# The experts' stage of a retention and mixture-of-experts kernel, written as a list of single steps per expert

## The chip, the cores and the metric

The kernel runs on one core of a Trainium2 chip. The core has TensorE for matmuls (PE in the profile, with its weight loads as PEld), VectorE (DVE), ScalarE (ACT), GpSimd (POOL) and SyncE (SP), which here only issues DMAs. Each engine works through its own queue in order, and an instruction that waits holds up everything behind it in its queue. SBUF holds the operands; PSUM, with eight banks of 512 floats per partition, takes the results of matmuls. The metric is the device time of one execution in microseconds (us).

## The reference

Retention attention over 8 batches, 8 heads, 576 tokens of 64 elements gives a matrix x of 4608 tokens by 512. Each token then goes to the one expert of eight whose embedding it is most like, and the output is that expert's two-layer network, scaled by the gate:

```
scores = (q @ k.T) / 8;  ret = scores * gamma_h ** (i - j) (j <= i, else 0);  x = ret @ v
logits = (x / |x|) @ (emb / |emb|).T / tau
idx = argmax(logits);  gate = softmax(logits)[idx]
for e in range(8):
    m = idx == e
    h = relu(x[m] @ w1[e])            # 512 -> 1024
    out[m] = gate[m] * (h @ w2[e])    # 1024 -> 512
```

All of it is float32.

## The kernel before

**Stages.** Attention and routing come first, batch after batch. Then the experts follow one after another, each with a capacity of 640 tokens in five tiles of 128. Expert 0's first layer is multiplied plainly; the experts 1 to 7 use Strassen's seven products with the tokens in two halves. A last part for tokens beyond capacity runs only if there are any.

**Precision.** Each float32 operand of the experts is split in two: ScalarE writes the rounded high part, and another engine then subtracts it from the source for the low part. A product is three matmuls, high by high, high by low and low by high. So each weight and each activation costs a ScalarE copy and a subtraction.

**An expert.** Its tokens are gathered by an indirect DMA that GpSimd issues (`gather`, line 404). `xturn` (453) lays the two 16-bit halves of each float apart on VectorE (457) and SyncE starts a transposing DMA (458); `xjoin` (462) joins them again on ScalarE (465) and forms the differences for Strassen in three VectorE instructions (479). `xput_b` and `xput_t` split the two results into `xsb` and `xst` (429, 430). The first layer's weights come in four loads; `sums1` forms block sums (218, four VectorE instructions) and `part1` splits them (226 and 227) into one of three slots. The second layer's weights come in four loads too, and `split2` splits them (191 and 192): the subtraction stands on GpSimd for experts 1 to 7.

**Rounds.** The first layer runs in four rounds. `round_a(r)` issues products 1 and 5 of block r and products 7 and 3 of block r-1; `round_b(r)` issues 6 and 2 of r and 4 of r-1. Products share banks: ScalarE copies bank z to x (1099), q to SBUF (1100) and z to v (1103) in between, and VectorE adds (1104, 1114). Each finished half goes through `out_half`: ScalarE's Relu (981), then VectorE's low part (982). A z bank is used by every other round, so it must be read to the end by then.

**Second layer.** `mm2` (1000) makes one tile of 128 tokens from 24 matmuls of 512 columns. `mm2_out` scales it by the gate on ScalarE (1013) and GpSimd scatters it with an indirect DMA (1017). Tiles 0 to 4 use banks m, o, m, o, m. Tile 4's matmuls are split: half of them before the next expert's `round_a(0)` and half behind it.

**Order.** From expert 0's second layer on, under `tc.manual_schedule()`, each engine takes instructions in the order in which the code is written. Work for the next expert is put between the rounds through the lists `bg`, `bg0`, `bg1`, `ahead` and `fill`. Buffers named raw are seven, for gathers, weight loads and block sums alike; a load or gather waits until one is free. Attention's part is ordered by a scheduler.

Of the kernel before, what the change touches and what calls it, by code (L numbers as in the profile page):

```python
# [9 lines left out]
F32 = mybir.dt.float32  # L10
# [3 lines left out]
U16 = mybir.dt.uint16  # L14
# [36 lines left out]
S1, S2, S3, S4, A11, A12, A22 = range(7)  # L51
PRODUCTS = {
# [54 lines left out]
def retention_moe(ctx: ExitStack, tc: tile.TileContext, qk, kv, embT, tau, w1, w2, cst, out):  # L107
# [344 lines left out]

    def xturn(e, i):

        t = xg[e, i]
        far = t[:, XO : XO + DM]
        nc.vector.tensor_copy(planes(far), words(t[:, :DM]))  # L457
        nc.sync.dma_start_transpose(
            out=t[:, :DM].bitcast(U16).rearrange("p (c n) -> p c n", n=P), in_=far.bitcast(U16)
        )  # L460

    def xjoin(e, i):
# [3 lines left out]
        if e == 0:  # L466
            return
        u = t[:, XO : XO + DM].rearrange("p (d n j) -> p d n j", d=NP, n=2)
        v = t[:, :DM].rearrange("p (k d n j) -> p k d n j", k=2, d=2, n=2)
        for o, x, y in (  # L470
# [8 lines left out]
            nc.vector.tensor_tensor(out=o, in0=x, in1=y, op=ALU.subtract)  # L479

# [486 lines left out]
    with ExitStack() as moe:  # L967
# [108 lines left out]
        def split2(e, c):  # L1076

            w_split(raws.pop((e, 1, c)), 1, c, nc.gpsimd if e else nc.vector)
# [15 lines left out]
        def round_a(e, r, width, bg=()):  # L1094

            products(e, width, [(1, r), (5, r)] * (r < 4) + [(7, r - 1), (3, r - 1)] * (r > 0))
            if r < 4:
                z, q = bank["z"][r % 2], half5[:, r % 2]
                nc.scalar.copy(bank["x"][:, :HALF], z[:, :HALF])  # L1099
                nc.scalar.copy(q, bank["q"][:, :HALF])  # L1100
            if r > 0:
                z, q = bank["z"][1 - r % 2][:, :HALF], half5[:, 1 - r % 2]
                nc.scalar.copy(bank["v"][:, :HALF], z)
                nc.vector.tensor_tensor(out=z, in0=z, in1=q, op=ALU.add)  # L1104
                for f in bg:
                    f()
                out_half(4 + r - 1, 1, z)
                out_half(r - 1, 1, bank["y"])

        def round_b(e, r, width, bg0=(), bg1=()):  # L1110

            products(e, width, [(6, r), (2, r)] * (r < 4) + [(4, r - 1)] * (r > 0))
            if r < 4:
                nc.vector.tensor_tensor(
                    out=bank["y"][:, :HALF], in0=bank["z"][r % 2][:, :HALF], in1=half5[:, r % 2], op=ALU.add
                )
            for f in bg0:
                f()
            if r < 4:
                out_half(r, 0, bank["x"])  # L1120
            if r > 0:
                out_half(4 + r - 1, 0, bank["v"])
            for f in bg1:
                f()
# [17 lines left out]
        for f in range(4, NF):  # L1142
            done = mm1_out(f, 0, mm1_in(f, 0))
            with after(*done):
                if f == 4:
                    gates()
                elif f == 5:
                    gates_out()
                    xturn(0, 3)
                    xturn(0, 4)  # L1150
                    gather(1, 0)
                elif f == 6:
                    count_beyond()
                    gather(1, 1)
                elif f == 7:
                    gather(1, 2)
                    gather_gates(0)
                split2(0, f - 4)

        with tc.manual_schedule():  # L1160
            ps = mm2(0, 0, fs=range(NF))
            xjoin(0, 3)
            xput_b(0, 3)
            xjoin(0, 4)
            xput_b(0, 4)
            gather(1, 3)
            gather(1, 4)
            gather_gates(1)
            for i in range(3):
                xturn(1, i)  # L1170
            load(1, 0, 0)
            mm2_out(0, 0, ps)
            ps = mm2(0, 1, fs=range(NF))
            for i in (3, 4):
                xturn(1, i)
            for i in (0, 1):
                xjoin(1, i)
                xput_t(1, i)
# [299 lines left out]
```

## Time and profile before

| | us |
|---|---|
| median of 3 runs | 672.48 (667.14 to 675.56) |
| the profiled execution | 673.74 |
| its span, first to last instruction | 671.9 |
| PE busy | 595.1 (89%) |
| DVE busy | 469.4 (70%) |
| ACT busy | 327.7 (49%) |
| POOL busy | 252.0 (38%) |
| mean granted clock of TensorE | 0.958 |

In the profile a line such as L1099 is that line of the kernel before. An entry "A <- B" says that A waited and B ended the wait. Matmuls overlap by about 0.16 us at the seams of the timeline's groups, so a group's cost is the distance from its start to the next group's start. Expert 0's second layer starts at 191.6 us, expert 1's first product at 238.9, and the experts 2 to 7 start at 298.6, 359.9, 422.1, 480.9, 544.6 and 606.2. The last tile of the expert that starts at 422.1 holds too few tokens to need its 24 matmuls, and they are skipped.

### The profile page before, as it was taken

Reading aid. Unit: us, or ns where it says so; the run is one execution under the profiler, and the core shown is the slowest. Engines: PE = TensorE matmul, PEld = TensorE weight load, DVE = VectorE, ACT = ScalarE, POOL = GpSimd, SP = SyncE. Lnnn points to the kernel's source line nnn. Section 1 sums busy time; section 2 is a strip of 40 time slices with the busy share of each in tenths; the row PEclk is TensorE's granted clock in tenths of the full one; section 3 lists DMA queues with packets and bytes.
Section 4 is the critical chain, followed back from the end, with each engine's and each line's share of the span. In section 5 each row is a group of like instructions: output and inputs, shape, how many; then the busy total and the mean of one; then the engine's idle time right before and its main releaser. Section 6 shows DMA issues by size and latency. Waiting matters only on the chain. (4 is left out here: it accounts for less than half of the span.)

```text
span 671.9 us, 13104 instructions
## 1 busy us (share of the span) xinstructions
PE 595.1 (89%) x5081; PEld 514.6 (77%) x5081; DVE 469.4 (70%) x966; ACT 327.7 (49%) x581; POOL 252.0 (38%) x193
## 2 busy tenths in 40 slices
PE   8999999997996898897889698987969897989796
PEld 7778778776886797687768686975768687769685
DVE  5676778787584878776886869577767859685700
ACT  1034324323563664664395457546734855575411
POOL 1422210221365045066325715650572257053311
PEclk9999999999999797999999898989989898989899
DMA  8898988847256255453734546364545344562001
GB/s 306 316 328 306 364 322 298 306 158 234 82 131 153 75 188 128 105 185 114 142 99 160 127 96 202 116 101 114 182 107 130 125 145 125 95 214 78 1 32 42
DMA packets 73299, 109.75 MB, mean 163 GB/s; under 512 B 44631, under 2 KB 45051, under 8 KB 71424
## 3 DMA queue, kind: packets, MB, share of 16 engines
q1 hardware_dynamic: 65536, 88.63, 42.9%
q0 software_dynamic: 7680, 19.95, 10.1%
q8 instruction: 60, 0.98, 0.6%
q14 instruction: 23, 0.19, 0.1%
HBM read 79.96 MB, written 19.94 MB: 149 GB/s over the span
## 5 line engine op out<-in xcount | busy, mean ns | idle before, releaser
L1000 PE MATMUL m<-wslot,hs 128*128 128x512 f32 (+1 forms) x888 | 209.7, 393 | 16.2 <-ACT y L1013 12.2
L1000 PEld LDWEIGHTS m<-wslot,hs 128*128 128x128 f32 x888 | 164.7, 192 | 55.4 <-ACT y L1013 14.8
L1017 POOL DMA_INDIRECT out<-y,sid x40 | 43.2, 1079 | 232.5 <-ACT y L1013 172.4
L1051 PE MATMUL a<-xst,wslot 128*128 128x292 f32 (+2 forms) x504 | 90.1, 323 | 20.3 <-ACT o L1099 14.3
L1051 PEld LDWEIGHTS a<-xst,wslot 128*128 128x128 f32 x504 | 79.5, 206 | 25.2 <-ACT o L1099 15.7
L227 DVE TENSOR_TENSOR wslot<-raw,wslot 128x768 fp32r<-128x768 f32 (+1 forms) x56 | 80.6, 1458 | 4.0 <-ACT wslot L226 3.7
L457 DVE COPY raw<-raw 128x1024 uint16<-128x1024 uint16 x37 | 53.9, 1458 | 36.9 <-DMA raw<-xd,gid 36.9
L192 POOL TENSOR_TENSOR wslot<-raw,wslot 128x1024 fp32r<-128x1024 f32 x28 | 66.7, 2400 | 21.0 <-ACT wslot L191 20.8
L658 POOL TENSOR_TENSOR vt<-vt,cs 128x512 f32<-128x512 f32 x28 | 28.4, 1046 | 87.5 <-DMA vt<-kv 57.5
L408 POOL DMA_INDIRECT raw<-xd,gid x40 | 47.3, 1182 | 33.5 <-DVE raw L690 20.3
L226 ACT CAST wslot<-raw 128x768 fp32r<-128x768 f32 (+1 forms) x56 | 50.6, 940 | 16.0 <-DVE raw L218 16.0
L419 POOL DMA_INDIRECT gt<-gd,gid x40 | 50.0, 1251 | 12.2 <-issue 10.7
L465 ACT COPY raw<-raw 128x1024 uint16<-128x1024 uint16 x37 | 49.8, 1347 | 4.4 <-DMA raw<-raw 4.4
L129 PE MATMUL a<-qkt 64*128 64x128 f32 (+1 forms) x640 | 46.9, 275 | 3.1 <-DVE raw L690 1.8
L479 DVE TENSOR_TENSOR raw<-raw 128x128 f32<-128x128 f32 (+1 forms) x105 | 35.3, 336 | 16.5 <-ACT raw L465 13.7
L129 PEld LDWEIGHTS a<-qkt 64*128 64x128 f32 (+1 forms) x640 | 38.3, 176 | 9.1 <-DVE raw L690 3.0
L690 DVE TENSOR_TENSOR raw<-a,tri 128x512 f32<-128x512 f32 x64 | 41.3, 681 | 5.5 <-PE a L129 5.4
L981 ACT ACTIVATE hs<-a 128x320 fp32r<-128x320 f32 (+2 forms) x44 | 19.1, 437 | 52.6 <-DVE a L1104 43.7
L1013 ACT ACTIVATE y<-m,gt 128x512 f32<-128x512 f32 (+1 forms) x38 | 25.7, 676 | 39.0 <-PE m L1000 38.8
L218 DVE TENSOR_TENSOR raw<-raw 128x256 f32<-128x256 f32 x112 | 42.4, 420 | 1.7 <-DMA raw<-w 0.6
L1051 PE MATMUL a<-xsb,wslot 128*128 128x292 f32 (+2 forms) x168 | 28.5, 305 | 13.0 <-DVE hs L982 12.3
L129 PE MATMUL a<-xsb,wslot 128*128 128x384 f32 (+1 forms) x192 | 31.7, 325 | 8.5 <-DVE hs L982 8.5
(164 smaller groups left out, 982.2 us busy)
## 6 DMA issues: line engine op xcount, KB each, us to landing
raw<-w SPq DMA_DIRECT2D x64, 512.0 KB, 4.5
qkt<-qk SPq DMA_DIRECT2D x32, 576.0 KB, 6.7
xd<-y SPq DMA_DIRECT2D x36, 256.0 KB, 3.1
vt<-kv SPq DMA_DIRECT2D x7, 1152.0 KB, 9.7
kt<-kv SPq DMA_DIRECT2D x7, 1024.0 KB, 5.2
vt<-kv SPq DMA_DIRECT2D x4, 256.0 KB, 7.9
raw<-xd,gid POOLq DMA_INDIRECT x40, 4.3
gt<-gd,gid POOLq DMA_INDIRECT x40, 3.7
```

Source lines behind the costliest of these rows:

```text
L129: pe[:] = [nc.tensor.matmul(*args, **kw)]
L192: (eng or nc.vector).tensor_tensor(out=sl[:, 1, c * 1024 : (c + 1) * 1024], in0=raw, in1=hi.bitcast(F32), op=ALU.subtract)
L218: nc.vector.tensor_tensor(out=o, in0=x, in1=y, op=op)
L226: nc.scalar.copy(sl[:, 0, b0:b1], src)
L227: nc.vector.tensor_tensor(out=sl[:, 1, b0:b1], in0=src, in1=sl[:, 0, b0:b1].bitcast(F32), op=ALU.subtract)
L408: return nc.gpsimd.indirect_dma_start(out=t[:, :DM], out_offset=None, in_=xd[:rows, :], in_offset=bass.IndirectOffsetOnAxis(ap=gid[:, a : ...
L419: nc.gpsimd.indirect_dma_start(out=g[:, i : i + 1], out_offset=None, in_=gd[:, :], in_offset=bass.IndirectOffsetOnAxis(ap=gid[:, a : a + 1 ...
L457: nc.vector.tensor_copy(planes(far), words(t[:, :DM]))
L465: nc.scalar.copy(words(t[:, XO : XO + DM]), planes(t[:, :DM]))
L1000: nc.tensor.matmul(ps[:, :step], hs[:, hsp, f, i * P : (i + 1) * P], w[:, ws, f, n : n + step], start=(part[0] and f == fs[0] and k == 0), ...
L1017: nc.gpsimd.indirect_dma_start(out=out[:, :], out_offset=bass.IndirectOffsetOnAxis(ap=sid[:, a : a + 1], axis=0), in_=y, in_offset=None, b ...
L1051: nc.tensor.matmul(ps[:, :n], w[:, ws, blk, d], x[:, xsp, d0 + d, half, :n], start=(new and d == 0 and k == 0), stop=(d == 1 and k == 2), ...
```

## The change

Rounds and background lists are replaced by three texts of words, `FIRST` (from expert 0's second layer to expert 1), `SECOND` (expert 1) and `SCHED` (experts 2 to 7). `walk` goes through a text, and `step` issues one word's instructions: A and B the products of a round, cx, cq, cv the copies, sy, sz the sums, h.. and l.. ScalarE's high part and VectorE's low part of one piece, a the block sums, M.. the second layer's matmuls, y the scaled output. A + marks work for the next expert: g a gather, u the laying apart, d its transposing DMA, j the joining, s the differences, w and v weight loads, G the gathers of gates. What used to be issued together, a high part and its low part, or u and d, is now placed word by word.

Besides the order, three things change. `split2`'s subtractions go to VectorE for all experts. The five output tiles use banks m, o, x, v, m. And the three first-layer banks are cleared only from column 292 on.

```diff
+SCHED = """
+A0 +g0 a3 cx0 Mz4 cq0 h20 h22 l20 B0 l22 yz4 +g1 h21 sy0 +g2 A1 hx0 lx0 l21 cx1 +g3 h23 cq1 l23 cv0
+sz0 +g4 B1 hz0 hy0 lz0 ly0 sy1 hx1 +u0 +d0 A2 hv0 hr3 lx1 cx2 lv0 hs3 lr3 cq2 cv1 sz1 B2 hz1 ls3 hy1
...
-            w_split(raws.pop((e, 1, c)), 1, c, nc.gpsimd if e else nc.vector)
+            w_split(raws.pop((e, 1, c)), 1, c)
...
+        def minus(out, x, y):
+
+            nc.vector.tensor_tensor(out=out, in0=x, in1=y.bitcast(F32), op=ALU.subtract)
...
+            elif k in ("h2", "l2"):
+                raw = raws[e, 1, i]
+                h, l = w2_parts(i, raw)
+                if k == "h2":
+                    nc.scalar.copy(h, raw)
+                else:
+                    minus(l, raw, h)
+                    del raws[e, 1, i]
+            elif k in MPART:
+                fs, part = MPART[k]
+                o = e - (k == "Mz")
+                ps = bank["moxvm"[i]]
+                mm2(o, i, ps, fs, part, wide[o] if i == CT - 1 and o else None)
...
-                ps = mm2(e, 2, bank["m"])
-                mm2_out(e, 2, ps)
...
+                for t in (*bank["z"], bank["q"]):
+                    nc.vector.memset(t[:, WIDTHS[0] : HALF], 0.0)
...
+        def walk(text, e):
+
+            for word in text.split():
+                (step if e or word[0] == "+" else opening)(word, *[e] * (e > 0 or word[0] == "+"))
...
         with tc.manual_schedule():
+            walk(FIRST, 0)
             for e in range(1, NE):
+                walk(SCHED if e > 1 else SECOND, e)
+                if e < NE - 1:
+                    walk("Mc4", e)
```

**VectorE in the first rounds of an expert.** This is VectorE's queue from the first sum of an expert's round 0 before; slots named wslot_84 and wslot_2771 hold the first layer's weights, and the COPY is the laying apart for the next expert.

```order
L1114 TENSOR_TENSOR m<-a,half_2772 128x320
L1034 UNCONDITIONAL_BRANCH
L982 SCALAR_TENSOR_TENSOR hs<-o,hs 128x5x64
L218 TENSOR_TENSOR raw<-raw 128x256 x4
L1034 UNCONDITIONAL_BRANCH
L1104 TENSOR_TENSOR a<-a,half_2772 128x320
L982 SCALAR_TENSOR_TENSOR hs<-a,hs 128x5x64
L982 SCALAR_TENSOR_TENSOR hs<-m,hs 128x5x64
L1114 TENSOR_TENSOR m<-a,half_2772 128x320
L457 COPY raw<-raw 128x1024
L1034 UNCONDITIONAL_BRANCH
L982 SCALAR_TENSOR_TENSOR hs<-o,hs 128x5x64 x2
```

The same stretch now, for an expert under `SCHED`; wslot_2769 is the second layer's weights, and L1170, L1220, L1147, L252 and L1186 are the lines of a split, a sum, a low part of the activations, the block sums and the laying apart:

```order
L252 TENSOR_TENSOR raw<-raw 128x256 x4
L1170 TENSOR_TENSOR wslot_2769<-raw,wslot_2769 128x1024 x2
L1220 TENSOR_TENSOR m<-a,half_2772 128x320
L1147 SCALAR_TENSOR_TENSOR hs<-o,hs 128x5x64
L1080 UNCONDITIONAL_BRANCH
L1170 TENSOR_TENSOR wslot_2769<-raw,wslot_2769 128x1024 x2
L1080 UNCONDITIONAL_BRANCH
L1220 TENSOR_TENSOR a<-a,half_2772 128x320
L1147 SCALAR_TENSOR_TENSOR hs<-a,hs 128x5x64
L1147 SCALAR_TENSOR_TENSOR hs<-m,hs 128x5x64
L1220 TENSOR_TENSOR m<-a,half_2772 128x320
L1186 COPY raw<-raw 128x1024
```

The block sums of the last weight load moved ahead of the first sum, and the four subtractions for the second layer's weights, which stood on GpSimd, now stand around it. The first COPY keeps its place behind round 1's sum.

**TensorE at the second layer of an expert.** The queue before, with the numbers of the banks (3266 is m, 3267 is o):

```order
L1000 MATMUL m_3267<-wslot2_2769,hs_2768 128x512 x18
L1000 MATMUL m_3266<-wslot2_2769,hs_2768 128x512 x6
L1000 MATMUL m_3267<-wslot2_2769,hs_2768 128x512 x6
L1000 MATMUL m_3266<-wslot2_2769,hs_2768 128x512 x24
L1000 MATMUL m_3267<-wslot2_2769,hs_2768 128x512 x24
```

The queue now, where m is 3052, o is 3053, x is 3274 and v is 3275:

```order
L1046 MATMUL m_3053<-wslot2_2769,hs_2768 128x512 x18
L1046 MATMUL m_3052<-wslot2_2769,hs_2768 128x512 x6
L1046 MATMUL m_3053<-wslot2_2769,hs_2768 128x512 x6
L1046 MATMUL o_3274<-wslot2_2769,hs_2768 128x512 x24
L1046 MATMUL o_3275<-wslot2_2769,hs_2768 128x512 x24
```

The order of TensorE's matmuls stays; tiles 2 and 3 are written to two banks that the first layer no longer needs at that point, instead of to those of tiles 0 and 1.

**GpSimd at the start of expert 0's second layer.** The gathers of tokens are L408 and those of gates L419 before:

```order
L268 TENSOR_TENSOR ss_all<-ss_all,half 128x36
L408 DMA raw<-xd,gid 128x512 x6
L419 DMA gt<-gd,gid 128x1 x5
L408 DMA raw<-xd,gid 128x512
L419 DMA gt<-gd,gid 128x1 x5
L1017 DMA out<-y,sid 4608x512 x4
```

Now they are L442 and L453:

```order
L302 TENSOR_TENSOR ss_all<-ss_all,half 128x36
L442 DMA raw<-xd,gid 128x512 x7
L453 DMA gt<-gd,gid 128x1 x10
L1063 DMA out<-y,sid 4608x512 x4
L1080 UNCONDITIONAL_BRANCH x2
```

All seven gathers of tokens now stand ahead of the ten gathers of gates; the seventh used to stand behind five of them.

More of the change, by code (lines that the diff above doesn't have):

```diff
@@ L479, in xjoin @@
             nc.vector.tensor_tensor(out=o, in0=x, in1=y, op=ALU.subtract)
+    def xjoin(e, i):
+        joined(e, i)
+        if e:
+            folded(e, i)
     def xput_t(e, i):
@@ L1092, in count @@
             return nc.tensor.value_load(ovt[0:1, e : e + 1], min_val=0, max_val=HALF)
[L1094 to L1108, printed above, removed]
@@ L1110, in round_b, with hi, lo, w2_parts @@
-        def round_b(e, r, width, bg0=(), bg1=()):
-            products(e, width, [(6, r), (2, r)] * (r < 4) + [(4, r - 1)] * (r > 0))
-            if r < 4:
+        def hi(src, f, n):
+            nc.scalar.activation(hs_half(0, f, n), five(src), AF.Relu)
+        def lo(src, f, n):
+            h = hs_half(0, f, n)
+            nc.vector.scalar_tensor_tensor(
+                out=hs_half(1, f, n), in0=five(src), scalar=0.0, in1=h.bitcast(F32), op0=ALU.max, op1=ALU.subtract
+            )
+        def w2_parts(c, raw):
+            return (late["w2"][:, k, c * 1024 : (c + 1) * 1024] for k in range(2))
@@ new lines, in w1_parts, with x_parts @@
+        def w1_parts(e, j, k):
+            sl = w1_slot(e, j)
+            b0, b1, src = (4, 7, raws[e, 0, j][:, 256:]) if k == "r" else (0, 4, sums[e, j])
+            return src.rearrange("p (b n) -> p b n", n=256), sl[:, 0, b0:b1], sl[:, 1, b0:b1]
+        def x_parts(e, i, k):
+            src = xg[e, i][:, :DM] if k == "t" else xg[e, i][:, XO : XO + DM]
+            dst = late["xst"] if k == "t" else xsb
+            src = src.rearrange("p (r n j) -> p r n j", r=NP, n=2)
+            return (src,) + tuple(dst[:, s, :, :, i * Q : (i + 1) * Q] for s in range(2))
@@ L1163, in retention_moe @@
[L1163 to L1178, printed above, removed]
-            mm2_out(0, 1, ps)
-            ps = mm2(0, 2, fs=range(NF))
@@ L1201, in retention_moe @@
-            bank["x"], bank["v"] = (pso.tile([P, 512], F32, name="o") for _ in range(2))
-            bank["y"], bank["m"], bank["o"] = (psm.tile([P, 512], F32, name="m") for _ in range(3))
-            ps = mm2(0, 3, bank["y"], fs=range(NF))
-            for i in range(CT):
-                xput_b(1, i)
-            bank["z"] = [psa.tile([P, 512], F32, name="a") for _ in range(2)]
-            bank["q"] = psa.tile([P, 512], F32, name="a")
-            for t in (*bank["z"], bank["q"]):
-                nc.vector.memset(t, 0.0)
@@ L1210, in retention_moe @@
-            part1(1, 1, 0)
-            load(1, 0, 2)
-            mm2_out(0, 3, ps)
-            part1(1, 1, 1)
-            w = count(1)
-            mm2(0, 4, bank["m"], range(4), (True, False))
-            load(1, 1, 0)
-            load(1, 1, 1)
-            round_a(1, 0, w)
-            sums1(1, 2)
-            part1(1, 2, 0)
-            part1(1, 2, 1)
-            ps = mm2(0, 4, bank["m"], range(4, NF), (False, True))
-            mm2_out(0, 4, ps)
-            def fill(*steps):
-                return [lambda g=g, a=a: g(*a) for g, *a in steps]
@@ L1300, in retention_moe @@
+            walk(FIRST, 0)
+            for e in range(1, NE):
+                walk(SCHED if e > 1 else SECOND, e)
+                if e < NE - 1:
+                    walk("Mc4", e)
+            e = NE - 1
+            y = None
+            for c in (0, DM // 2):
+                ps = mm2(e, CT - 1, bank["o" if c else "m"], width=wide[e], n=c, step=DM // 2)
+                y = mm2_out(e, CT - 1, ps, y, c, DM // 2)
     ntile = nc.values_load(ovt[0:1, 0:1], min_val=0, max_val=NO)
```

253 lines of the change are left out of this document (143 added, 110 removed).

## The prediction

> **What bounds the kernel now.** I read the windows by stage first, then TensorE's waits, then the timelines of one ordinary expert. In the windows, the columns are the stretch, its length, the busy time of PE, PEld, DVE, ACT and POOL, the granted clock, and the DMAs' share and rate.
>
> ```profile
> 191.60:238.90 47.30, 38.60 (x207) 33.57 (x207) 32.97 (x80) 25.65 (x37) 17.66 (x17) 0.89 0.53 136
> 238.90:298.57 59.67, 54.78 (x289) 48.37 (x289) 48.38 (x85) 37.78 (x62) 25.28 (x16) 0.94 0.55 147
> 298.57:359.87 61.30, 52.98 (x289) 46.48 (x288) 46.23 (x79) 35.95 (x61) 29.31 (x21) 0.97 0.49 130
> 359.87:422.08 62.21, 54.44 (x289) 47.22 (x288) 46.43 (x79) 36.13 (x61) 28.93 (x21) 0.95 0.50 135
> 422.08:480.90 58.82, 50.99 (x277) 43.87 (x275) 43.05 (x76) 34.46 (x58) 25.04 (x17) 0.97 0.53 124
> 480.90:544.64 63.74, 54.79 (x276) 48.25 (x277) 48.06 (x81) 37.60 (x62) 30.17 (x21) 0.92 0.50 137
> 544.64:606.17 61.53, 54.49 (x289) 47.30 (x288) 46.29 (x78) 36.07 (x60) 27.18 (x19) 0.94 0.51 135
> 606.17:671.90 65.73, 54.83 (x325) 49.69 (x323) 21.03 (x30) 20.79 (x41) 16.36 (x11) 0.96 0.10 36
> ```
>
> TensorE is the busiest engine in every expert, and no engine is busy throughout. The seven experts last 433.0 us and TensorE is busy for 377.3 of it; the difference is 55.7. The last group of matmuls tells how much of that is the tail behind it, 671.9 - 665.8 = 6.1:
>
> ```profile
> 642.19 23.63 PE L1000 MATMUL m<-wslot,hs 128*128 128x512 f32 x126
> ```
>
> So TensorE waits for 49.6 us inside the experts. The view of its waits (total, times, longest) says for whom:
>
> ```profile
> PE a L1051 <- ACT o L1099: 14.3, 6, 5.4
> PE a L1051 <- DVE hs L982: 12.3, 6, 4.4
> PE m L1000 <- ACT y L1013: 12.2, 6, 2.0
> PE a L129 <- DVE hs L982: 8.5, 1, 8.5
> ```
>
> The first two are the rounds: a bank or a low part that ScalarE or VectorE hands over late. The third is a tile of the second layer that waits for its bank. The fourth lies in the opening. Expert 2 on TensorE:
>
> ```profile
> 298.57 0.96 PE L1051 MATMUL a<-xsb,wslot 128*128 128x292 f32 x6
> 299.37 0.97 PE L1051 MATMUL a<-xst,wslot 128*128 128x292 f32 x6
> ...
> 317.55 1.40 PE L1051 MATMUL a<-xst,wslot 128*128 128x292 f32 x6 [4.03 <-ACT o L1099]
> ...
> 346.14 13.89 PE L1000 MATMUL m<-wslot,hs 128*128 128x512 f32 x60 [2.01 <-ACT y L1013]
> ```
>
> A product costs 0.80 (299.37 - 298.57), a matmul of 512 columns 13.89 / 60 = 0.2315. An expert has 28 products and 120 such matmuls: 22.4 + 27.8 = 50.2 us, against some 61 that it takes.
>
> Why the 4.03? VectorE and GpSimd in the same microseconds:
>
> ```profile
> 312.40 4.21 DVE L457 COPY raw<-raw 128x1024 uint16<-128x1024 uint16 x1 [2.32 <-DMA raw<-xd,gid]
> ...
> 317.32 3.35 DVE L227 TENSOR_TENSOR wslot<-raw,wslot 128x768 fp32r<-128x768 f32 x1
> ...
> 321.00 0.68 DVE L457 COPY raw<-raw 128x1024 uint16<-128x1024 uint16 x1
> 321.60 0.48 DVE L982 SCALAR_TENSOR_TENSOR hs<-a,hs 128x320 fp32r<-128x320 f32 x1
> ...
> 322.58 0.50 DVE L1114 TENSOR_TENSOR m<-a,half 128x320 f32<-128x320 f32 x1
> 322.99 1.22 DVE L227 TENSOR_TENSOR wslot<-raw,wslot 128x1024 fp32r<-128x1024 f32 x1
> 324.12 0.88 DVE L982 SCALAR_TENSOR_TENSOR hs<-o,hs 128x320 fp32r<-128x320 f32 x2
> ```
>
> ```profile
> 311.34 4.70 POOL L192 TENSOR_TENSOR wslot<-raw,wslot 128x1024 fp32r<-128x1024 f32 x2
> ...
> 317.46 2.38 POOL L192 TENSOR_TENSOR wslot<-raw,wslot 128x1024 fp32r<-128x1024 f32 x1
> ```
>
> VectorE first waits 2.32 for a gather, with the round's work queued behind. Its copy then takes 4.21, though the same copy takes 0.68 at 321.00: it ends when GpSimd's two subtractions do (316.04). The subtraction at 317.32 is held the same way until 319.84. Two causes, then: a gather taken up too early, and GpSimd's arithmetic.
>
> After a long wait the clock falls as well:
>
> ```profile
> 318.00:320.00 2.00, 2.00 (x11) 2.00 (x10) 2.00 (x1) 0.18 (x1) 1.85 (x1) 0.52 1.12 207
> 346.00:348.00 2.00, 1.86 (x8) 1.56 (x9) 1.34 (x3) 2.00 (x4) 1.27 (x1) 1.00 0.66 240
> 408.00:410.00 2.00, 2.00 (x6) 1.52 (x6) 0.88 (x3) 2.00 (x3) 0.26 (x1) 0.50 0.50 199
> ```
>
> Length times (1 - clock), summed over the seven experts' windows, is 21.7 us. Part of it falls into the waits themselves, where it costs nothing. I take 17, with 14 and 20 as bounds.
>
> **The change part by part.** *GpSimd's subtractions go to VectorE*: four per expert at 1.13 (322.99 to 324.12) add 4.5 us there, and the holding of 4.21 - 0.68 and 3.35 - 0.95 goes. Whether VectorE still fits is the main question. More spacings:
>
> ```profile
> 342.83 1.08 DVE L479 TENSOR_TENSOR raw<-raw 128x256 f32<-128x256 f32 x3
> ...
> 350.05 1.55 DVE L218 TENSOR_TENSOR raw<-raw 128x256 f32<-128x256 f32 x4
> 352.12 0.69 DVE L430 TENSOR_TENSOR xst<-raw,xst 128x512 fp32r<-128x512 f32 x1
> ...
> 352.72 4.09 DVE L227 TENSOR_TENSOR wslot<-raw,wslot 128x768 fp32r<-128x768 f32 x4
> ```
>
> From first product to second layer (A0 to Ma0), TensorE has 27 products and 12 matmuls, 21.6 + 2.8 = 24.4 us. VectorE has 13 low parts at 0.40 and 7 sums at 0.41 (8.1), four splits (4.5), one set of block sums (1.5), one weight's two low parts (2.0, half of 4.09), five layings apart at 0.60 (3.0) and one set of differences (1.0): 20.1. From there to the next expert TensorE has 108 matmuls and a product, 25.8; VectorE three block sums (4.4), three weights (6.0), ten halves of tokens at 0.60 (6.0), four sets of differences (4.0) and the last round (1.6): 22.0. So VectorE is filled to 82% and 85%. ScalarE's work stays, 35.95 in expert 2's row, 72% of 50.2.
>
> Averages hide round trips, so I followed both queues through an expert. With A0 at 0, A1 is due at 6.0, A2 at 11.6, A3 at 17.2. The tightest place is bank z before A3: product 7 of round 1 ends at 14.2, ScalarE copies q and v to 14.9, VectorE adds to 15.4, subtracts the weight's second part to 16.5 and reads z to 16.9, 0.3 ahead of TensorE. Elsewhere the lead is 0.3 to 0.6. I therefore take 0.7 us of waits per expert for experts 2 to 6; bounds are 0 and, if every handover took 0.1 more, 2. Expert 7 prepares nothing: 0.5.
>
> Expert 1 (`SECOND`) must still do the third weight, 3.5 us more before Ma0 and no differences: 22.6 of 24.4. The same walk has z read at 11.9 for an A2 due at 11.6, and at 18.7 for an A3 due at 17.6. I take 3 us, between 0 and its present 4.9.
>
> *The layings apart move behind their gathers.* A gather takes
>
> ```profile
> raw<-xd,gid POOLq DMA_INDIRECT x40, 4.3
> ```
>
> us to land. The first is issued at A0 and its copy comes at 11.7; the last is issued after the fourth split at 9.7, its copy comes at 22.4. The transposing DMAs follow their copies one by one on SyncE, ahead of the weight load w0 in that queue; their joins come 4 to 10 us later. If they land late, ScalarE stalls, but at that point TensorE has the second layer's matmuls. This term costs nothing unless landing takes twice as long.
>
> *Five banks.* Tiles 2 and 3 no longer wait for ScalarE's y of tiles 0 and 1: 12.2 us go. What is late next there is the Relu of the last round; in the walk it is done 2 us ahead. Banks x and v are wanted back only by cx0 and cv0, and y2 and y3 stand ahead of these on ScalarE. The smaller clears save under 1 us on VectorE, hidden.
>
> *The opening.* Before:
>
> ```profile
> 203.13 0.94 POOL L408 DMA_INDIRECT raw<-xd,gid  x1 [0.30 <-issue]
> ...
> 208.50 0.69 DVE L457 COPY raw<-raw 128x1024 uint16<-128x1024 uint16 x1 [6.42 <-DMA raw<-xd,gid]
> ...
> 221.69 9.23 PE L129 MATMUL a<-xsb,wslot 128*128 128x256 f32 x60 [8.47 <-DVE hs L982]
> ```
>
> One gather stands behind five gate gathers, VectorE waits 6.42 for it, the backlog runs into expert 0's low parts and TensorE waits 8.47. Now the gather stands ahead, and the expert's own low parts come between single steps. TensorE's idle time there, 47.30 - 38.60 = 8.7, goes, and about 2 us of cold clock with it; I put back 2.
>
> **The sum.** Span 671.9, less 49.6 of waits, 17 of cold clock, 8.7 and 2 in the opening: 594.6, the floor. Back come 3 (expert 1), 3.5 (2 to 6), 0.5 (7), 2 (opening) and 3 of cold clock behind these: 606.6. The profiled execution took 673.74, 1.84 over its span, and the median of the runs is 1.3 below it: 606.6 + 1.8 - 1.3 = 607.
>
> The clock term deserves a doubt. The three rows show half clock after 4.03 us of waiting, full clock after 2.01 (346), half after 2.04 (408): a wait of 2 us may or may not do it. The Trainium skill (TensorE: Matmul & The Clock Gate, Part 1) has the clock halve only after an idle window of about 3.4 us; by it only three or four long waits would have cost, some 6 us, and the sum would be 618. The 408 row speaks against that.
>
> **The rivals.** *The rounds stay short of VectorE and ScalarE* (12%). If handovers take 0.4 us longer than I read them, each of four rounds waits about 1 us and the clock falls now and then: some 5 us per expert, 7 x 5 = 35, 642; with 3 or 6 it is 622 to 650. For it: leads of only 0.3. Against: the long wait of expert 2, at 317.55, stands behind a held copy, not behind a slow handover.
>
> *The change does not deliver* (6%): buffers come free late, because gathers 1 to 4 each need a split to end first, and the copies wait as before. Then the banks' 12.2 and the opening go and the rounds stay: 672 - 12 - 9 = 651, up to no change, 650 to 672. Against: the 7 us of margin above.
>
> *Slower: VectorE becomes the bound* (4%). If GpSimd's DMA instructions hold VectorE as its arithmetic does, 15 of them per expert at 1.2 us add 18 to VectorE's 42.1. That makes 60 of its own and some 63 with handovers, 1.8 over today's mean of 61.2: 7 x 1.8 = 13, 685. It decides once VectorE needs over 60 us per expert. Against it stands the row at 352.72: four subtractions in 4.09, the free rate, beside this gate gather:
>
> ```profile
> 353.37 1.16 POOL L419 DMA_INDIRECT gt<-gd,gid  x1 [0.30 <-issue]
> ```
>
> The Trainium skill (GPSIMD Engine Reference, 1. Specifications) says that GpSimd shares its SBUF interfaces with VectorE's instructions of two SBUF inputs, the kind that is moved here. For arithmetic this trace agrees (3.35 at 317.32); for DMA instructions the row above does not.
>
> **How the numbers follow.** Forecast 75% (597 to 622 of its own, by the bounds above), the first rival 12%, the second 6%, slower 4%; 3% for a span below the forecast's own range. The range 597 to 632 takes in the forecast and half of the first rival, about 8 in 10. A change of 2% is about what a measurement of this kernel can tell from none: faster means below 659. That holds for the forecast, the first rival and part of the second: 0.91. Within 2%: 0.05. Slower: 0.04.
>
> **What would show it.** Right: PE busy over 96% in experts 2 to 6 with starts 51 to 53 us apart, no L457 or L227 successor above 1.3 us, no wait of tile 2 for y, mean clock above 0.98, a single small wait in the opening. Wrong: TensorE waiting on cx or on low parts by over 2 us per expert (first rival), VectorE waiting for gathers (second), VectorE's subtractions above 1.3 us with GpSimd issuing DMAs (third), or clocks of 0.5 without long waits (the clock term).

## The result, and the profile after

The changed kernel takes 600.2 us (median of 4 runs, 597.9 to 601.8) against 674.0 for the kernel before: a ratio of 0.892, 95% interval 0.885 to 0.899. Forecast were 607, with 597 to 632 as the range. The profiled execution took 600.29 us, its span is 598.11. One run each of three kernels below was in a slow state (614.9, 623.6 and 1114.4 us) and is left out of their medians here, which is why two expectations name 610.8 and 639.9 where the table has 609.8 and 638.4.

The windows by stage of the changed kernel, with the same columns as before (stretch, length, busy time of PE, PEld, DVE, ACT, POOL, granted clock, DMAs' share and rate). The first row is everything ahead of expert 0's second layer, the second the opening, the others are experts 1 to 7. Ahead of them stands the one row of the kernel before that was not shown yet, for its first stretch:

```profile
0.00:191.60 191.60, 179.21 (x2847) 149.87 (x2848) 136.97 (x383) 63.30 (x141) 52.10 (x52) 0.99 0.74 269
```

```profile
0.00:195.45 195.45, 181.76 (x2848) 152.62 (x2849) 136.71 (x383) 63.42 (x141) 52.12 (x52) 0.98 0.73 264
195.45:231.50 36.05, 36.05 (x207) 31.74 (x207) 30.79 (x79) 25.02 (x37) 17.76 (x16) 1.00 0.62 154
231.50:283.73 52.23, 51.25 (x290) 45.91 (x289) 47.26 (x89) 37.27 (x61) 16.60 (x14) 1.00 0.64 184
283.73:334.57 50.84, 50.47 (x289) 45.10 (x288) 45.33 (x88) 36.59 (x62) 17.94 (x15) 1.00 0.63 172
334.57:385.19 50.62, 50.31 (x290) 45.07 (x289) 42.73 (x83) 35.80 (x60) 18.16 (x15) 1.00 0.58 160
385.19:435.04 49.85, 47.72 (x278) 42.60 (x276) 41.72 (x80) 35.87 (x60) 17.95 (x15) 1.00 0.64 157
435.04:487.68 52.64, 50.37 (x276) 44.98 (x277) 44.15 (x86) 35.63 (x60) 16.46 (x15) 1.00 0.59 155
487.68:538.95 51.27, 50.30 (x289) 45.06 (x288) 42.66 (x82) 35.81 (x60) 17.83 (x15) 1.00 0.60 160
538.95:598.11 59.16, 53.03 (x325) 48.47 (x323) 17.55 (x30) 20.89 (x41) 8.56 (x8) 0.99 0.09 33
```

Three things are to be read here. An ordinary expert (2 to 6) now lasts 49.9 to 52.6 us where it lasted 58.8 to 63.7, and TensorE is busy in nearly all of it. The granted clock is 1.00 throughout the experts, but for the tail of the last. And VectorE's busy time per expert has fallen although it took four subtractions over: 42.7 in expert 3, where it was 46.4.

TensorE's waits in the changed kernel (total, times, longest), the rows of the experts:

```profile
PE a L1097 <- DVE m L1220: 3.0, 4, 1.5
PE a L1097 <- DVE hs L1147: 1.7, 5, 0.9
PE a L1097 <- ACT y L1059: 1.5, 1, 1.5
PE a L1097 <- ACT half L1215: 0.7, 1, 0.7
```

The waits for bank x (14.3 us), for bank m (12.2) and the one in the opening (8.5) are gone. Where the 73.8 us of span went: 66.4 out of the experts (433.0 before, 366.6 now), 11.25 out of the opening (47.30, now 36.05), and 3.85 were lost in the stretch ahead of it. That loss can't be put down to the change: the stretch ends between 190.8 and 195.6 us in the fourteen traces of this document, at 191.0 and 194.5 in two kernels of the old order, at 190.8 and 195.6 in two of the new one.

### The profile page after: what moved, and what is told of

Its sections match the earlier page's. It is cut to its first block, busy times and chain, and to the rows that moved or that the text cites. A ratio compares the mean times of both kernels' runs of the same rounds, so it can differ in the third digit from the quotient of the medians.

```text
span 598.1 us, 13075 instructions
## 1 busy us (share of the span) xinstructions
PE 571.2 (96%) x5081; PEld 501.6 (84%) x5081; DVE 448.9 (75%) x994; ACT 326.3 (55%) x581; POOL 183.4 (31%) x165
## 5 line engine op out<-in xcount | busy, mean ns | idle before, releaser
L1046 PE MATMUL m<-wslot,hs 128*128 128x512 f32 (+1 forms) x576 | 130.5, 381 | 0.0
L1063 POOL DMA_INDIRECT out<-y,sid x40 | 50.7, 1268 | 237.6 <-ACT y L1059 129.3
L1046 PEld LDWEIGHTS m<-wslot,hs 128*128 128x128 f32 x576 | 103.9, 188 | 19.6
L1170 DVE TENSOR_TENSOR wslot<-raw,wslot 128x768 fp32r<-128x768 f32 (+1 forms) x84 | 93.8, 1130 | 20.6 <-ACT wslot L1230 17.1
L1046 PE MATMUL o<-wslot,hs 128*128 128x512 f32 x384 | 88.6, 389 | 0.0
L1046 PEld LDWEIGHTS o<-wslot,hs 128*128 128x128 f32 x384 | 72.0, 188 | 14.9
L1097 PE MATMUL a<-xst,wslot 128*128 128x292 f32 (+2 forms) x504 | 80.0, 300 | 3.8 <-DVE m L1220 3.0
L442 POOL DMA_INDIRECT raw<-xd,gid x40 | 45.3, 1133 | 40.3 <-DVE raw L736 20.3
L736 DVE TENSOR_TENSOR raw<-a,tri 128x512 f32<-128x512 f32 x64 | 41.3, 681 | 6.9 <-PE a L163 6.9
L453 POOL DMA_INDIRECT gt<-gd,gid x40 | 42.4, 1059 | 12.2 <-issue 11.6
L252 DVE TENSOR_TENSOR raw<-raw 128x256 f32<-128x256 f32 x112 | 42.5, 420 | 1.2
L881 ACT COPY y<-m 128x512 f32<-128x512 f32 x34 | 18.9, 586 | 32.6 <-PE m L167 32.5
L163 PE MATMUL o<-raw,vt 128*64 128x128 f32 x512 | 35.6, 278 | 0.0
```

What stands on the lines that cost most here:

```text
L163: pe[:] = [nc.tensor.matmul(*args, **kw)]
L252: nc.vector.tensor_tensor(out=o, in0=x, in1=y, op=op)
L442: return nc.gpsimd.indirect_dma_start(out=t[:, :DM], out_offset=None, in_=xd[:rows, :], in_offset=bass.IndirectOffsetOnAxis(ap=gid[:, a : ...
L453: nc.gpsimd.indirect_dma_start(out=g[:, i : i + 1], out_offset=None, in_=gd[:, :], in_offset=bass.IndirectOffsetOnAxis(ap=gid[:, a : a + 1 ...
L736: nc.vector.tensor_tensor(out=pm[:, h], in0=ps[h].rearrange("p (c n) -> p c n", c=NCH), in1=tri.unsqueeze(1).broadcast_to([P, NCH, P]), op ...
L1046: nc.tensor.matmul(ps[:, :step], hs[:, hsp, f, i * P : (i + 1) * P], w[:, ws, f, n : n + step], start=(part[0] and f == fs[0] and k == 0), ...
```

## The experiments

Each kernel was timed beside the kernel before on the same chip; the ratios are to that one. Its own median was 674.0 to 677.0 in these rounds, so where a difference is under some 4 us I look at the trace too: the time from the start of expert 0's second layer to the end leaves out the spread ahead of it. In the order of the argument:

| kernel | us, median | ratio, 95% interval |
|---|---|---|
| changed kernel | 600.2 | 0.892 (0.885 to 0.899) |
| changed, w2's subtractions on GpSimd | 644.8 | 0.962 (0.956 to 0.969) |
| before, w2's subtractions on VectorE | 634.0 | 0.948 (0.940 to 0.955) |
| the same, with five banks | 638.4 | 0.942 (0.936 to 0.948) |
| the same, layings apart later | 621.0 | 0.919 (0.915 to 0.922) |
| changed, banks m and o alone | 610.7 | 0.908 (0.900 to 0.916) |
| changed, two layings apart earlier | 602.3 | 0.891 (0.887 to 0.894) |
| changed, gathers 3 and 4 later | 599.4 | 0.887 (0.882 to 0.892) |
| changed, opening's gathers behind the gates' | 599.9 | 0.888 (0.884 to 0.892) |
| changed, opening's steps grouped | 603.8 | 0.894 (0.889 to 0.898) |
| changed, w2's subtractions done twice | 623.5 | 0.923 (0.918 to 0.928) |
| changed, y first, first try | 609.8 | 0.910 (0.903 to 0.916) |
| changed, y first, second try | 596.2 | 0.881 (0.878 to 0.885) |

### GpSimd's arithmetic, from both sides

My theory: GpSimd's subtractions hold VectorE, and that is the larger cause. The rival: VectorE's load, or the new order, is what counts. First the changed kernel with that one part undone:

```diff
                 else:
-                    minus(l, raw, h)
+                    minus(l, raw, h, nc.gpsimd)
                     del raws[e, 1, i]
```

(and `minus` takes the engine as an argument)

> The changed kernel with one thing undone: the low parts of the four w2 chunks are subtracted on GpSimd again, at the places that they have in the new lists. Theory (GpSimd's arithmetic holds VectorE): in the profile before the change such a subtraction took 2.38 us on GpSimd, and VectorE's copy beside it 4.21 in place of 0.68, its subtraction of two operands in SBUF 3.35 in place of 0.95. VectorE then gains 4 x 1.2 us per expert and loses up to 2.4 for each of the four that falls beside such work, always inside the rounds, where its lead is 0.3 to 0.7 us; I expect 3 to 6 us more per expert with the clock that falls behind longer waits, 620 to 645 us against 600, copies (line 1186) and low parts (line 1170) above 1.5 us on average beside GpSimd, and the clock under 0.98. Rival (VectorE's load is the limit, and the new places alone did it): VectorE has 4.8 us less to do per expert, and the time is 595 to 603.

It came to 644.8 us, at the edge of what the theory gave; the rival is out. VectorE, GpSimd and TensorE in the rows that show it:

```profile
305.90 0.50 DVE L1220 TENSOR_TENSOR m<-a,half 128x320 f32<-128x320 f32 x1
307.85 3.58 DVE L1186 COPY raw<-raw 128x1024 uint16<-128x1024 uint16 x1 [1.45 <-DMA raw<-xd,gid]
311.35 0.88 DVE L1147 SCALAR_TENSOR_TENSOR hs<-o,hs 128x320 fp32r<-128x320 f32 x2
```

```profile
308.52 2.35 POOL L1170 TENSOR_TENSOR wslot<-raw,wslot 128x1024 fp32r<-128x1024 f32 x1
```

```profile
312.38 1.31 PE L1097 MATMUL a<-xst,wslot 128*128 128x292 f32 x6 [3.42 <-ACT o L1213]
```

The copy that takes 0.68 alone takes 3.58 and ends 0.6 behind GpSimd's subtraction; the low parts of the round stand behind it, and TensorE waits 3.42 for the bank that they free. My number for the sizes was too bold in one place: copies and low parts were to be above 1.5 us on average. They are at 1.18 (copies) and 1.47 (low parts of 1024), and the clock is 0.972.

Then the kernel before with that one line changed, everything else as it was:

```diff
-            w_split(raws.pop((e, 1, c)), 1, c, nc.gpsimd if e else nc.vector)
+            w_split(raws.pop((e, 1, c)), 1, c, nc.vector)
```

> The kernel before with one line changed: the four low parts of w2 per expert are subtracted on VectorE, everything else stays, the coarse groups and the places of the gathers too. Theory (the hold is the larger cause of the rounds' waits, and gathers queue behind GpSimd's 2.4 us of arithmetic): the copies go from 1.46 us on average to 0.7 (37 of them, 28 us) and the 28 subtractions of 768 from 1.69 to 0.95 (21 us), against 28 x 1.2 = 34 us more of subtractions; with the gathers earlier, I expect 640 to 655 against 673, while the 12 us of waits for bank m and the 8.5 in the opening stay. Rival (the groups are what matters): VectorE is loaded as much as before, and whole groups still stand ahead of the rounds' work; 665 to 680.

634.0 us, better than expected: one line brings 40 of the 74 us. The groups of VectorE's instructions (busy time, mean ns of one, idle time before them), in the kernel before and then in this one:

```profile
L227 DVE TENSOR_TENSOR wslot<-raw,wslot 128x768 fp32r<-128x768 f32 x28 | 47.4, 1693 | 2.0 <-ACT wslot L226 1.6
L457 DVE COPY raw<-raw 128x1024 uint16<-128x1024 uint16 x37 | 53.9, 1458 | 36.9 <-DMA raw<-xd,gid 36.9
```

```profile
L227 DVE TENSOR_TENSOR wslot<-raw,wslot 128x768 fp32r<-128x768 f32 x28 | 26.6, 948 | 1.4 <-ACT wslot L226 1.2
L457 DVE COPY raw<-raw 128x1024 uint16<-128x1024 uint16 x37 | 25.3, 685 | 12.7 <-DMA raw<-xd,gid 12.3 <-issue 0.4
```

On average the copies are back at 0.69 us and these subtractions at 0.95, the times that they have alone, and two thirds of the waits for gathers are gone too, which fits that the gathers no longer stand behind 2.4 us of arithmetic in GpSimd's queue. How the 40 us divide between the two, this run doesn't tell.

### The banks, and a wait that moves

In the changed kernel, back to two banks:

```diff
-                ps = bank["moxvm"[i]]
+                ps = bank["momom"[i]]
```

(and the same in the line that evicts them)

> The changed kernel with one thing undone: the five tiles of the second layer use the banks m and o in turn again (m, o, m, o, m) in place of five. Theory (the third tile's wait was a term of its own): TensorE waits for y0 ahead of tile 2 again, 2.03 us in six experts, 12 us, and another 0 to 6 us for a clock that falls; 612 to 618 against 600. Rival (it only gives VectorE the time that TensorE waits for elsewhere): of the 6 us that TensorE now waits in the rounds most goes, and the time is 604 to 608.

610.7, so 10.5 us (11 by the ratios), where I had 12 to 18; it lies between the two expectations. The wait for y0 is shorter here, 0.6 to 1.2 in place of 2.03 (5.3 us in all), and the sum into y is late by 1.0 to 1.4 behind it (6.0 in all, 3.0 in the changed kernel). It is a term of its own, a little smaller than I wrote it.

The same step on the side of the kernel before, on top of the one-line change:

```diff
-                ps = mm2(e, 2, bank["m"])
+                ps = mm2(e, 2, bank["x"])
...
-                ps = mm2(e, 3, bank["o"])
+                ps = mm2(e, 3, bank["v"])
```

> The kernel before with two things done: the w2 subtractions on VectorE (634.0 us alone) and tiles 2 and 3 of the second layer in the banks x and v; the coarse groups and the opening stay. Theory (the two add up, as they sit at different places): the 10.6 us of waits for y0 that are left go, 621 to 625. What then remains to the changed kernel's 600 is the opening and the spreading in single steps, about 10 each. Rival (VectorE's groups are late next): the wait moves to the Relu or the first round behind it, 630 to 635.

638.4: no gain over 634.0 (the intervals of the ratios overlap). The wait moved, as the rival had it, and the time is 3 us beyond even the rival's range. Waits of TensorE, then the rows of VectorE and of GpSimd ahead of one of them, and the last scatter of the next expert:

```profile
PE a L1051 <- ACT o L1099: 18.0, 6, 4.5
```

```profile
307.23 1.22 DVE L192 TENSOR_TENSOR wslot<-raw,wslot 128x1024 fp32r<-128x1024 f32 x1
311.77 0.69 DVE L457 COPY raw<-raw 128x1024 uint16<-128x1024 uint16 x1 [3.32 <-DMA raw<-xd,gid]
312.38 0.88 DVE L982 SCALAR_TENSOR_TENSOR hs<-o,hs 128x320 fp32r<-128x320 f32 x2
```

```profile
307.07 0.98 POOL L1017 DMA_INDIRECT out<-y,sid  x1 [4.39 <-ACT wslot L191]
308.36 0.99 POOL L408 DMA_INDIRECT raw<-xd,gid  x1 [0.30 <-issue]
...
363.61 0.98 POOL L1017 DMA_INDIRECT out<-y,sid  x1 [4.22 <-DMA out<-y,sid]
```

The 10.6 us for y0 are gone, and 18.0 us for bank x stand in their place: the first gather is still queued on GpSimd behind the output scatter of the last tile, and VectorE waits 3.32 for it with the low parts behind. TensorE's arrival two microseconds earlier is only part of it. Counted from the expert's first product, the gather is issued at 14.3 us here (308.36 - 294.08) and at 10.6 with two banks (305.25 - 294.70 in that trace): the last two scatters begin 5.4 us apart here and 3.5 there, and the row at 363.61 says that such a scatter waits for the landing of the one before. Why that takes longer here is open. So this is the prediction's second cause, a copy that stands too early for its gather, but by a gather that has become later. The changed kernel has its first gather ahead of that scatter in GpSimd's queue (`+g0` ahead of `yz4`), which no run tested alone. The next step leaves the gathers and moves the layings apart half a round to a round later, in the same kernel:

```diff
-                round_b(e, 1, w, fill((split2, e, 2)) + list(ahead((xturn, n, 0))), fill((part1, e, 3, 0)))
+                round_b(e, 1, w, fill((split2, e, 2)), fill((part1, e, 3, 0)))
...
-                round_a(e, 2, w, ahead((xturn, n, 1)))
+                round_a(e, 2, w)
...
-                round_b(e, 2, w, fill((part1, e, 3, 1)), fill((split2, e, 3)) + list(ahead((xturn, n, 2))))
+                round_b(e, 2, w, fill((part1, e, 3, 1)), fill((split2, e, 3)) + list(ahead((xturn, n, 0))))
...
-                round_a(e, 3, w, ahead((xturn, n, 3)))
+                round_a(e, 3, w, ahead((xturn, n, 1)))
-                round_b(e, 3, w, ahead((xturn, n, 4)), ahead((sums1, n, 0)))
+                round_b(e, 3, w, ahead((xturn, n, 2)), ahead((xturn, n, 3), (sums1, n, 0)))
-                round_a(e, 4, w)
+                round_a(e, 4, w, ahead((xturn, n, 4)))
```

> The kernel before with the w2 subtractions on VectorE, five banks, and the five layings apart each half a round to a round later (the first behind B2's low parts in place of B1's sum). Without that last step it came to 639.9, slower than without the banks (634.0): a wait of 3.5 us for bank x had taken the place of the 2.03 for y0, as VectorE's first copy waited 3.32 for a gather. Theory (a gather taken up too early was the second cause, as the prediction has it): the waits of VectorE for gathers go from 20.9 us to under 10, TensorE's 18.0 us for bank x mostly go with the clock behind them; 612 to 622. Rival (the gathers come too late whatever stands ahead of them, as they queue on GpSimd behind the scatter of the last tile): the wait moves with the copies, 632 to 642.

621.0: 17 us less. VectorE's waits for gathers are 7.8 us (6.4 of it one wait in the opening), TensorE's for bank x 2.7. Three edits to the old, coarse order thus give 53 of the 74 us. What is left to 600.2 is in the trace 10.2 us in the opening (expert 1 begins at 241.74 here, at 231.50 in the changed kernel) and 12.7 in the experts (379.3 against 366.6).

### Places of gathers and layings apart in the new order

```diff
-... cv1 sz1 B2 hz1 ls3 hy1 lz1 ly1 +w0 sy2 hx2 +u1 +d1 A3 hv1 lx2 lv1 +u2 +d2 +u3 +d3 cx3 ...
+... cv1 sz1 +u1 +d1 B2 hz1 ls3 hy1 lz1 ly1 +w0 sy2 hx2 +u2 +d2 A3 hv1 lx2 lv1 +u3 +d3 cx3 ...
```

> The changed kernel with two layings apart of experts 3 to 7 back where the kernel before had them: the second in A2 behind the sum into z, the third in B2 behind y's sum (half a round earlier each). Theory (that place is worth something in the new order too): the second gather is issued 11 us behind A0 and takes 5.9 to land, the copy at 16 waits about 1 us, ahead of the low part that frees z for A3; TensorE waits 1 us more per expert, 603 to 608. Rival (single steps and prompt gathers make the place indifferent): 598 to 602.

602.3. The trace shows the wait that the theory named, ahead of A3 (0.77 to 0.88 in four experts, 0.15 to 0.27 with the copies later, and 3.48 once, in expert 5), but the time lies between the two expectations and its interval overlaps that of the changed kernel. From expert 0's second layer to the end its trace takes 406.0 us against 402.7. The place is worth 0 to 3 us here, against 17 in the old order.

```diff
-... cx1 +g3 h23 cq1 l23 cv0 sz0 +g4 B1 ... +u0 +d0 A2 ... lz1 ly1 +w0 sy2 ...
+... cx1 h23 cq1 l23 cv0 sz0 B1 ... +u0 +d0 +g3 A2 ... lz1 ly1 +g4 +w0 sy2 ...
```

> The changed kernel with gathers 3 and 4 of experts 2 to 7 issued where the kernel before issued them: 3 ahead of A2, 4 behind B2, and the layings apart left at their new places. Theory (the gathers' earlier issue is only margin, the waits of 36.9 us came from GpSimd's arithmetic in their queue): VectorE's waits for gathers go from 2.9 to at most 10 us, half of it hidden; 600 to 606. Rival (the early issue carries the gain of the rounds): a copy waits 2 to 3 us in each of six experts ahead of the round's low parts, 615 to 625.

599.4, no difference; VectorE's waits for gathers are 2.0 us. The earlier issue of gathers 3 and 4 is margin only.

### The opening

```diff
-... H4 L3 +u0 +d0 +g3 L4 +u1 +d1 +g4 G0 +G0 N0 ...
+... H4 L3 +u0 +d0 L4 +u1 +d1 G0 +g3 +g4 +G0 N0 ...
```

> The changed kernel with the opening's gathers 3 and 4 for expert 1 behind the five gate gathers of expert 0, as one of them was before. Theory of the prediction (the gather's place made the 8.5 us wait): the copies of these two wait 2 to 5 us on VectorE, the first low parts of the opening's second half are late again, and TensorE waits 3 to 6 us: 604 to 608. Rival (the order of VectorE's single steps made it, the gather is hidden): TensorE waits under 1 us there, 599 to 602.

599.9, the rival's outcome. VectorE does wait, and nothing comes of it; the last row here is the same low part in the changed kernel:

```profile
211.09 0.69 DVE L1186 COPY raw<-raw 128x1024 uint16<-128x1024 uint16 x1 [3.19 <-DMA raw<-xd,gid]
...
214.42 0.41 DVE L1271 SCALAR_TENSOR_TENSOR hs<-a,hs 128x256 fp32r<-128x256 f32 x1
```

```profile
214.07 0.42 DVE L1271 SCALAR_TENSOR_TENSOR hs<-a,hs 128x256 fp32r<-128x256 f32 x1 [1.79 <-ACT hs L1269]
```

The first low part of the opening's second half comes 20.0 us behind the opening's start (194.40), against 18.6 in the changed kernel, where VectorE had 1.79 to spare at this place; only a subtraction, a copy and one set of differences stand between the late copy and it. In the kernel before:

```profile
221.21 0.42 DVE L982 SCALAR_TENSOR_TENSOR hs<-a,hs 128x256 fp32r<-128x256 f32 x1
```

The copy that waited 6.42 there ended at 209.2, and the first low part came 12 us behind it: the group of preparation steps between them was longer than the wait. So the next kernel leaves the gathers early and draws such a group together:

```diff
-... P0 +s0 P1 hp0 lp0 +ht0 +lt0 P2 hp1 lp1 +j1 P3 hp2 lp2 +j2 +s1 P4 hp3 lp3 +ht1 y0 P5 +s2 hp4 +j3 lp4 +a1 P6 ...
+... P0 +s0 P1 +ht0 +lt0 +j1 +s1 +ht1 +j2 +s2 +a1 P2 hp0 lp0 hp1 lp1 P3 hp2 lp2 P4 hp3 lp3 y0 P5 hp4 +j3 lp4 P6 ...
```

> The changed kernel with the opening's preparation steps between the first low parts of its second half drawn together ahead of the first of them (four folds' worth: three of block sums, one low part of tokens, one set of differences, 5.4 us on VectorE, with their steps on ScalarE); the gathers stay early. Theory (the order of VectorE's steps, not the gather's place, made the 8.5 us of the opening): the first low part comes about 6 to 9 us later than at 214.1, TensorE has three banks and waits from about 216 on, 4 to 6 us, 604 to 608. Rival (without a late gather the group is done in time): TensorE waits under 1 us there, 599 to 602.

603.8, at the edge of what the theory gave. The time alone doesn't settle it, as the interval of its ratio overlaps that of the changed kernel; the trace does. TensorE's wait is back, of the kind it was and less than half as long:

```profile
219.47 8.56 PE L163 MATMUL a<-xsb,wslot 128*128 128x256 f32 x60 [3.72 <-DVE hs L1271]
```

The opening lasts 41.3 us (194.75 to 236.04) in place of 36.05. The order of VectorE's steps makes that wait; the gather's place alone doesn't. That the 8.5 were this group and the late gather together fits both runs, but the two in one kernel weren't tried.

### How much room VectorE has

```diff
                 else:
                     minus(l, raw, h)
+                    minus(l, raw, h)
                     del raws[e, 1, i]
```

> The changed kernel with each low part of w2 subtracted twice over (the second time the same numbers again), 4 x 1.2 = 4.9 us more on VectorE per expert, all between A0 and Ma0. Theory (VectorE is filled to 82% there, 20.1 of 24.4, so the room is 4.3 us and is spread over gaps of 0.3 to 0.9): 25.0 of 24.4 no longer fits, TensorE waits 2 to 4 us more per expert, and 614 to 630 results. Rival (the room is larger than counted, as work moves on into the second layer's time): under 605.

623.5: of 7 x 4.9 = 34 us more work 23 show (21 by the ratios). An expert takes 53.3 to 55.6 us, most of them with a wait of 0.8 for the sum into y and one of 2.3 for a low part. In all:

```profile
PE a L1097 <- DVE hs L1147: 15.3, 10, 2.4
PE a L1097 <- DVE m L1220: 7.2, 7, 2.3
```

That is 17.8 us above the changed kernel's 4.7, and three stretches of 3.4 us at half clock behind such waits add 5.1. The reckoned room of 4.3 us in the first half was not there as one piece, or it would have hidden most of it; VectorE is the next limit, and close.

### A faster version

The largest wait left in the experts is TensorE's 3.0 us for the last sum into bank y (line 1220). VectorE has z's low part and y's low part ahead of it, but only the latter is needed for that sum. The first try turned the order on both engines:

```diff
-... cv2 sz2 B3 hz2 hy2 lz2 ly2 +j0 sy3 +u4 ...
+... cv2 sz2 B3 hy2 hz2 ly2 +j0 sy3 lz2 +u4 ...
```

(and the same in `SECOND`)

> The changed kernel with one order turned in each expert's last full round: VectorE takes y's low part and the next sum into y ahead of z's low part. In the changed kernel TensorE waits 3.0 us in all (four times, up to 1.5) for that sum ahead of the round's last product but one. Theory (VectorE's order is the limit there): that wait goes and nothing else is late, 597 us against 600, ratio 0.995. Rival (the next operand in the row is as late): the wait moves to another releaser, 600.

609.8, slower by some 10, which neither expectation had. ScalarE and TensorE, expert 3:

```profile
353.86 0.41 ACT L1217 COPY o<-a 128x320 f32<-128x320 f32 x1
358.08 0.44 ACT L1142 ACTIVATE hs<-m 128x320 fp32r<-128x320 f32 x1 [3.81 <-PE o L1097]
```

```profile
353.66 0.96 PE L1097 MATMUL m<-xsb,wslot 128*128 128x292 f32 x6
```

The product into y ends at 354.62, and its Relu starts 3.46 us later, in three other experts 1.1 to 1.9. ScalarE has nothing to do meanwhile, and of what this Relu reads only that product is recent. The row names a later product, into o, as what ended the wait, but in expert 2 the same Relu starts at 303.87, ahead of the end of the first product into o (304.36), so it isn't that one that it needs. In the changed kernel the same Relu comes second and doesn't wait. The second try puts it ahead of B3, where all engines pass a branch:

```diff
-... cv2 sz2 B3 hz2 hy2 lz2 ly2 +j0 sy3 +u4 ...
+... cv2 hy2 sz2 B3 hz2 ly2 +j0 sy3 lz2 +u4 ...
```

(and the same in `SECOND`)

> The changed kernel with y's Relu of the last full round ahead of the products of B3 on ScalarE, and the next sum into y ahead of z's low part on VectorE. The first try of this order, with the Relu behind the point where B3 begins, came to 610.8 in place of 597: there TensorE's signal for the product into y came 1.1 to 3.5 us after its end. Theory (that late signal belongs to the place behind the branch): here the Relu runs 0.1 to 0.4 us behind the product, the sum comes 1 us earlier and TensorE's 3.0 us of waits for it go; 597 to 598. Rival (the signal is late wherever ScalarE waits for this product first): TensorE waits 5 us or more for the sum, 605 to 611.

596.2 us, ratio 0.881 (0.878 to 0.885): the fastest, 593.6 to 597.0 in its runs against 597.9 to 601.8, and in the trace 399.4 us from expert 0's second layer to the end against 402.7. The same two engines:

```profile
354.80 0.44 ACT L1142 ACTIVATE hs<-m 128x320 fp32r<-128x320 f32 x1 [0.39 <-PE m L1097]
```

```profile
353.81 0.96 PE L1097 MATMUL m<-xsb,wslot 128*128 128x292 f32 x6
```

The Relu starts 0.03 behind the end of the product (353.81 + 0.96 = 354.77), and TensorE's waits for the sum fall from 3.0 to 0.3.

## Why the prediction was right, step by step

**The size.** Its sum was 606.6 of span; measured are 598.1. By its own terms:

| term | forecast | measured |
|---|---|---|
| waits left in experts 1 to 7 | 7.0 | 7.0 |
| cold clock in the experts, net | -14 (17 less, 3 back) | -23.9 |
| opening | -8.7 (8.7 and 2 less, 2 back) | -11.25 |
| ahead of the opening | 0 | +3.85 |

The waits left are 366.6 of length, less 353.45 of busy time (the seven rows) and 6.1 of tail. The cold clock is the fall of TensorE's busy time for the same products, 377.3 to 353.45. The mechanism was right and this term was mis-sized: the windows gave 21.7, and I took 17, as part of it would fall into waits. The drop measured is 23.9, with no half clock left in the experts but in the tail of the last. (The trace's record of the granted clock has 40.8 us at half clock in the seven experts before, so 20.4 lost; the other 3.5 I can't place.) The differences add up to the miss: 9.9 + 2.55 - 3.85 = 8.6, against 606.6 - 598.1 = 8.5. As the 3.85 lie within the spread of that stretch, part of the closeness is chance: without them the miss would be 12.4.

**The causes.** That GpSimd's subtractions hold VectorE, and hold the gathers in its own queue, is shown from both sides: 40 us by undoing it alone in the kernel before, 45 by putting it alone back. The gather taken up too early is shown in the old order (17 us); in the new one it is worth some 3 at most. The prediction gave a gather 4.3 us to land, and in the changed kernel it takes 5.9; but expert 3's first one is issued 6.7 us behind expert 2's first product (290.46 - 283.73), where the two kernels of the old order above had 10.6 and 14.3. That this is why the place matters less is argued, not shown. The two causes are not a sum: which of them TensorE meets depends on when it arrives.

**The banks.** 12.2 us were forecast to go; in the new order they are worth 10 to 11. The step that the Relu of the last round is late next there, and done 2 us ahead, held for the new order. For the old one it would have failed: there the wait went over to bank x, whole.

**The opening.** That the wait goes was right. The cause named first, the gather behind five gate gathers, was not enough by itself; the backlog that it "runs into" was the part that mattered.

**VectorE's budget.** 42.1 us per expert were forecast, 42.7 measured in expert 3 (41.7 to 45.3 in experts 2 to 6). The total was right, its division was not: 82% and 85% were forecast for the two parts, and expert 3 has 75% (18.89 of 25.29 us up to the second layer) and 94% (23.85 of 25.33 behind). As room it misled: 4.9 us more in the part with the gaps cost 3.3 per expert.

**Right by luck.** The 7.0 of waits were 3 for expert 1, 3.5 for experts 2 to 6 and 0.5 for 7. Measured (length less busy time) are 1.0, 6.05 and, beside the tail, none. The surplus lies at experts 4 and 5 (2.13 and 2.27), where the kernel skips the fifth tile's 24 matmuls, 5.6 us: two of the waits, 1.47 and 0.73, stand right where the two halves of these matmuls would have been. The walk through the queues had that tile in every expert.

**The doubt on the clock.** A sum of 618 was given for the case that only waits near 3.4 us cost clock. It fell: TensorE's busy time went down by 23.9, where that case allows some 6.

**The rivals.** The rounds staying short (642), no delivery (651) and VectorE as the bound (685) are all out. For the last, VectorE's subtractions of 1024 beside GpSimd's gathers took 1.23 at most, and the longest of the 35 copies took 0.92. The first would have come near with arithmetic left on GpSimd: then the same places give 644.8.

**The signs.** PE is busy for over 96% of experts 2, 3 and 6 and for 95.7% of 4 and 5; the starts are 49.9 to 52.6 us apart, the mean clock is 0.993, tile 2 doesn't wait for y, and TensorE doesn't wait in the opening.

## What to carry to other kernels

Where an instruction takes several times its usual duration, look for what another engine does in the same microseconds before reordering anything: one such line was more than half of this change. A wait that is taken away in an order of coarse groups comes back at the next operand that isn't ready, so undo the causes together, and judge each from both sides. And an engine that is busy for 84% of the time need not have 16% to give: here 4.9 us more per expert cost 3.3.

## What the runs showed of the chip

**The clock falls in steps of 3.4 us.** In seven traces (the kernel before, the changed kernel, w2 on GpSimd, one line, one line with five banks, two banks, y first) each stretch at half clock within the experts is 3.4 us long or twice or three times that; only the tail of the last is cut off by the end. Two windows of the kernel before, one on each side of such an end:

```profile
318.10:321.50 3.40, 3.40 (x16) 3.40 (x15) 3.40 (x3) 0.46 (x3) 3.13 (x2) 0.50 0.72 138
321.50:324.90 3.40, 2.24 (x14) 1.76 (x14) 3.30 (x7) 3.12 (x7) 0.70 (x2) 1.00 0.73 162
```

And two of the kernel with one line changed, behind waits of TensorE of 2.02 us (ahead of 335.5) and 2.05 us (ahead of 445.8):

```profile
335.50:338.90 3.40, 3.40 (x15) 2.83 (x16) 2.21 (x6) 3.29 (x5) 1.27 (x1) 1.00 0.58 217
446.90:450.30 3.40, 3.40 (x10) 2.61 (x9) 2.19 (x7) 3.25 (x5) 0.50 (x2) 0.51 0.30 118
```

A wait of the same length costs nothing here and 1.7 us there (half of 3.4). Over the seven traces all 17 waits from 3.4 us up were followed by half clock, 12 of 19 between 1.8 and 2.8, and none up to 1.7 that stood alone. The other seven traces add three of three and four of eight. The Trainium skill (TensorE: Matmul & The Clock Gate, Part 1) has a free-running window of about 3.4 us that must be idle. The length agrees with these stretches, and a free-running window would explain why equal waits differ; that a wait of 2 us can be enough speaks against a window that must be idle throughout. For a sum that means: count 1.7 us beside two of three waits of about 2 us.

**What holds VectorE.** Arithmetic of GpSimd on two operands in SBUF does (0.68 to 3.58), issuing gathers and scatters does not (35 copies between 0.67 and 0.92 in the changed kernel). The Trainium skill (GPSIMD Engine Reference, 1. Specifications) has the two engines share SBUF interfaces; the first half agrees with that.

**A late signal.** In the first try of the faster version, ScalarE saw the end of a product 1.1 to 3.5 us late, in four experts, when a Relu directly behind a branch waited for it, and 0.03 us behind it when the Relu stood ahead of the branch. Why is open: no run here separates the branch, the place of the wait and what else the two orders change.
